# Attention ahead of a gated mixture of experts: smaller first loads, batch 0 partly transposed on TensorE, batch 1's transposes ahead of the first weights, adds in two alternating accumulators

## The chip, the core and the metric

One Trainium2 chip; the kernel runs on one of its cores. The metric is the device time of one execution in microseconds (us). Runs of one kernel differ by some tenths of a per cent.

## What is computed

Grouped-query attention over 8 batches (16 query heads, 4 key and value heads, 384 positions, 64 columns each), whose result is the input `x` (3072 x 1024) of a two-level gate: one of 4 groups, then one of 4 experts in it, each expert with two 1024 x 1024 matrices. Cut to what matters:

```python
scores = scale * np.matmul(q, k.transpose(0, 1, 3, 2))
attn = np.exp(scores - np.max(scores, axis=-1, keepdims=True))
attn = attn / (np.sum(attn, axis=-1, keepdims=True) + 1e-09)
x = np.matmul(attn, v)                      # per batch and head
g_idx = np.argmax(x @ w_group, axis=1)      # group, with its softmax weight
e_idx = np.argmax(xg @ w_expert[g], axis=1) # expert in the group, likewise
out[tok_idx] = combined[:, None] * (np.maximum(xg @ w1[g, e], 0.0) @ w2[g, e])
```

## The kernel before, in words

The program goes batch by batch. A batch's attention (`Attn.run`) has 24 units, six per key head `g`. A unit has four score products into one of two "s" tiles of PSUM (`score`, L256), an exp on ScalarE (L262, into a tile `e` of 128 x 768 f32), four value products (`pv`, L275, into an "o" tile), and an add on VectorE into the group's running sum (`tail`, L288): `es = es + e[u]`, five adds in a row on one tile. `score` runs two units ahead of `pv`. After a group its outputs are copied to `xT` (ScalarE, or VectorE for group 1). There are nine buffers for `e`.

Keys and queries must lie transposed. Of batch 0, the first half of the keys and the first query group are cast and transposed on TensorE (`first_scores`, L223 and L228) and the rest by DMA transposes on SP's queue (`trans_q` L122, `trans_k` L127). Of later batches all is transposed by DMA: `before_attention(b)` issues those of batch b + 1. Queries are loaded and cast by POOL's queue (L91), keys and values by SP's (L87, L96); a copy of the keys with each column doubled (`dup_k`, L115) is made by POOL in a single buffer.

Behind the attention of batch b comes `block(b)`: the expert of batch b - 1 (`ffn_h` L486: four pairs of hidden columns with a ReLU each; `ffn_y` L495) on TensorE, and around it for batch b the sums over keys (`reduce_keys` L321 on VectorE, `sums` L330 on TensorE and a reciprocal), the normalisation (`normalise`, L340 and L345 on VectorE), casts, and the gate (`gate_logits` L361, `gate_softmax`). The gate also guesses the expert that most tokens of batch b + 1 will want, from the mean of its values (`sum_v` L102 on VectorE, `guess_mean` L372), so that its weights can be requested early: `pick` reads the choice into a register on POOL and requests both matrices (L439, L442), 2 MB each as written. For batch 0 this guess is made inside its own attention, behind units 1 to 4, and batch 1's transposes are issued behind unit 5. Batch 1's attention carries batch 0's sums, normalisation and gate between its units. A loop at the end serves tokens that chose otherwise; it runs zero times here.

The order on every engine is the order in which the program is written; nothing is reordered. Each queue is served in order too: what stands behind a waiting instruction waits with it. The dictionaries given to `Attn.run` say behind which unit a step stands:

```python
at[0].run({
    1: [first_guess],
    2: [do(guess, 0)],
    4: [first_pick, do(prepare_k, 1)],
    5: [do(before_attention, 0)],
}, at[1])
```

## Time and profile before

| | |
|---|---|
| median of three runs | 440.46 us (439.91 to 441.97) |
| the profiled execution | 440.67 us |
| its span, first to last instruction | 439.0 us |
| busy, share of the span | TensorE 85%, VectorE 74%, ScalarE 55%, POOL 9% |
| mean granted TensorE clock | 0.97 of full speed |
| moved by transfers | 78.06 MB, mean 178 GB/s |

The profile shows one execution. Times within it count from the start of its span. Busy shares are means over stages with different limits, so the timeline of each engine is of more use here: it lists instructions in order, with the idle time of the engine ahead of an instruction and what ended that idle time, in brackets. PE is TensorE, DVE is VectorE, ACT is ScalarE; a queue is named with a q (SPq). A number L288 is a line of the kernel.

### The profile page before, as it was taken

How to read it: one execution, taken by the hardware profiler on the slowest of the kernel's cores; microseconds unless marked ns; L12 is line 12 of the kernel's file. 1: busy time of each engine (PE TensorE's matmuls, PEld its weight loads, DVE VectorE, ACT ScalarE, POOL GpSimd, SP SyncE). 2: the span in 40 equal slices, each digit the busy share in tenths (PEclk: the TensorE clock that was granted, in tenths of full speed). 3: DMA queues.
4: the chain of work that ended last, by engine and by line, in shares of the span. 5: the costliest groups of instructions: out<-in, count | busy, mean ns of one | idle time of the engine just before them, and what ended most of it. 6: DMA issues, size and time to landing. Idle time of an engine off the chain costs nothing.

```text
span 439.0 us, 8662 instructions
## 1 busy us (share of the span) xinstructions
PE 372.0 (85%) x3491; PEld 193.9 (44%) x3491; DVE 325.0 (74%) x509; ACT 242.7 (55%) x323; POOL 39.2 (9%) x52
## 2 busy tenths in 40 slices
PE   2895067587989999998999898999999899989993
PEld 1352033143445444554455444544455545544551
DVE  3689229999669994999499975999499949995321
ACT  3276057451659534973589265953497358926220
POOL 5030020040010010100210021001010001000000
PEclk9999578898999999999999999999999999999998
DMA  8949999249979999899969998999989946971524
GB/s 205 210 69 192 205 190 170 74 84 235 210 225 184 196 218 264 148 192 208 261 155 206 193 216 209 210 186 230 259 141 184 215 103 144 221 137 48 169 49 98
DMA packets 73050, 78.06 MB, mean 178 GB/s; under 512 B 37769, under 2 KB 52105, under 8 KB 73009
## 3 DMA queue, kind: packets, MB, share of 16 engines
q0 software_dynamic: 24736, 39.65, 53.2%
q1 hardware_dynamic: 47920, 37.36, 35.2%
q8 instruction: 28, 0.46, 0.4%
q10 hardware_dynamic: 352, 0.48, 0.4%
q14 instruction: 14, 0.11, 0.1%
HBM read 89.21 MB, written 18.87 MB: 246 GB/s over the span
## 4 chain that ended last, share of the span: by engine, by line
DVE 37%; PE 37%; issue 8%; ACT 8%; DMA 5%; SPq 2%; POOL 1%; DVEq 0%; POOLq 0%; ACTq 0%
DVE e L288 24%; PE ps_s L495 12%; PE ps_s L486 10%; ACT e L262 6%; DVE red L321 5%; DMA qT<-q_raw 4%; PE ps_o L495 4%; PE ps_o L275 3%; PE ps_o L361 2%; SPq L127 2%; DVE xT L294 1%; DVE vsum L102 1%; PE ps_o L486 1%; PE ps_s L256 1%; ACT ot L510 1%
## 5 line engine op out<-in xcount | busy, mean ns | idle before, releaser
L288 DVE TENSOR_TENSOR e<-e 128x768 f32<-128x768 f32 x160 | 154.8, 975 | 33.3 <-ACT xT L296 15.5
L262 ACT ACTIVATE e<-ps_s 128x768 f32<-128x768 f32 x192 | 148.0, 819 | 37.1 <-PE ps_s L256 31.9
L275 PE MATMUL ps_o<-e,v_raw 64*64 64x384 f32 x1536 | 162.7, 498 | 0.6 <-ACT e L262 0.2
L256 PE MATMUL ps_s<-qT,kT 64*64 64x384 bf16 x768 | 71.0, 339 | 27.4 <-DMA qT<-q_raw 17.5
L486 PE MATMUL ps_s<-xb,w 128*128 128x384 bf16 x480 | 82.3, 330 | 0.0
L275 PEld LDWEIGHTS ps_o<-e,v_raw 64*64 64x64 f32 x1536 | 63.3, 137 | 28.5 <-issue 17.3
L256 PEld LDWEIGHTS <-kT 64*64 64x64 bf16 x768 | 32.8, 108 | 75.1 <-issue 70.5
L486 PEld LDWEIGHTS <-w 128*128 128x128 bf16 x512 | 49.5, 99 | 37.0 <-issue 5.9
L488 ACT ACTIVATE hT<-ps_s 128x768 bf16<-128x768 f32 x30 | 24.3, 810 | 61.8 <-PE ps_s L486 61.8
L495 PE MATMUL ps_s<-w,hT 128*128 128x512 bf16 x248 | 55.5, 379 | 0.0
L495 PEld LDWEIGHTS <-hT 128*128 128x128 bf16 x384 | 36.1, 98 | 43.6 <-ACT hT L488 1.9
L349 ACT CAST xb<-xT 128x768 bf16<-128x768 f32 x32 | 26.3, 829 | 15.6 <-DVE xT L345 15.6
L345 DVE TENSOR_TENSOR xT<-xT,rb 128x768 f32<-128x768 f32 x32 | 31.8, 994 | 1.6
L495 PE MATMUL ps_o<-w,hT 128*128 128x512 bf16 x136 | 32.2, 379 | 0.0
L340 DVE STREAM_TRANSPOSE rb<-inv 128x768 f32<-128x768 f32 x32 | 31.3, 977 | 1.0
L321 DVE TRANSPOSE_TENSOR_REDUCE red<-e 128x24 f32<-128x768 f32 x32 | 28.7, 948 | 0.0
L296 ACT COPY xT<-ps_o 128x768 f32<-128x768 f32 x24 | 19.1, 796 | 7.8 <-PE ps_o L275 7.8
L514 ACT ACTIVATE ot<-ps_s,we 128x1024 f32<-128x1024 f32 x14 | 15.6, 1115 | 12.6 <-PE ps_s L495 12.6
L439 POOL DMA_DIRECT2D w<-in_moe_w_dram x8 | 7.1, 883 | 172.4 <-DVE cw_all L430 118.9
L102 DVE TENSOR_REDUCE vsum<-v_raw 128x256 bf16<-128x1536 f32 x8 | 22.1, 2761 | 0.0
L416 ACT ACTIVATE ex<-sh 128x24 f32<-128x24 f32 x8 | 1.8, 223 | 33.4 <-DVE sh L411 33.4
L91 POOL DMA_DIRECT2D q_raw<-in_q_dram x7 | 6.2, 881 | 153.9 <-DMA qT<-q_raw 153.9
(95 smaller groups left out, 159.7 us busy)
## 6 DMA issues: line engine op xcount, KB each, us to landing
w<-in_moe_w_dram POOLq DMA_DIRECT2D x16, 2048.0 KB, 21.6
out_dram<-ot SPq DMA_DIRECT2D x42, 256.0 KB, 5.5
v_raw<-in_v_dram SPq DMA_DIRECT2D x16, 384.0 KB, 6.6
xb_scratch<-xb SPq DMA_DIRECT2D x8, 768.0 KB, 6.4
q_raw<-in_q_dram POOLq DMA_DIRECT2D x7, 768.0 KB, 11.8
k_raw<-in_k_dram SPq DMA_DIRECT2D x7, 384.0 KB, 4.1
out_dram<-ot SPq DMA_DIRECT2D x12, 128.0 KB, 2.4
w<-in_q_dram POOLq DMA_DIRECT2D x3, 192.0 KB, 9.1
```

The source lines that it names most:

```text
L102: nc.vector.tensor_reduce(out=t.rearrange("p (h d) -> p h d", d=D), in_=vraw[b].rearrange("p h (c d) -> p h d c", c=NC), axis=AX.X, op=ALU ...
L256: nc.tensor.matmul(out=sT[r * H2:(r + 1) * H2, s, :S], lhsT=kT[b][s * D:(s + 1) * D, (g // 2) * NC + c, ks], rhs=qT[b][s * D:(s + 1) * D, ...
L262: nc.scalar.activation(e.rearrange("p t (s x) -> p s t x", s=2), sT[:, :, :S].rearrange("p s (t x) -> p s t x", t=2), ACT.Exp, scale=scale)
L275: nc.tensor.matmul(out=oT[t * D:(t + 1) * D, r, :S], lhsT=vraw[b][r * H2:(r + 1) * H2, g, c * D:(c + 1) * D], rhs=self.e[u][r * H2:(r + 1) ...
L288: nc.vector.tensor_add(out=es, in0=es, in1=self.e[u])
L321: nc.vector.tensor_reduce(out=red[b][:, g].rearrange("p t j -> p (t j)"), in_=ess[b][g].rearrange("p t (j x) -> p (t j) x", x=32), axis=AX ...
L340: nc.vector.transpose(out=rb.rearrange("p k (j x) -> p (k j) x", x=32), in_=inv[b][:, ks].rearrange("p k j -> p (k j)").unsqueeze(2).to_br ...
L345: nc.vector.tensor_mul(out=x, in0=x, in1=rb)
L349: nc.scalar.copy(out=xb[b][:, ks, :], in_=xT[b][:, ks, :])
L486: nc.tensor.matmul(out=h[:, jj, :S], lhsT=w1[:, kq, (f0 + jj) * P:(f0 + jj + 1) * P], rhs=x[:, kq, :], start=(kq == 0), stop=(kq == KQ - 1))
L488: nc.scalar.activation(hT[:, f0:f0 + 2, :], h[:, :, :S], ACT.Relu)
L495: nc.tensor.matmul(out=y[:, nh, :], lhsT=hT[:, f, c * P:(c + 1) * P], rhs=w2[:, f, nh * HALF:(nh + 1) * HALF], start=(f == 0), stop=(f == ...
```

## The change

Four things are done. First, the start: of the keys, the first half is loaded first, and of the values the first group; the second half of the keys and batch 1's keys and values are loaded behind them (`load_v0`). POOL builds the identity before it requests queries. ScalarE runs an exp on a constant at once (`early`). TensorE multiplies a constant eight times (`warm`). The first query group is cast, transposed and copied in two halves on two engines, and the second query group is transposed on TensorE as well (`first_q1`, behind unit 3). Second, batch 1's transposes, in four pieces for the queries, are issued ahead of batch 0's choice, which moves from behind unit 4 to behind unit 16; the value means of batches 0 and 1 are made by TensorE from the values themselves (`guess_mean_pe`, twelve products of 128 x 128 f32 with a column of ones) instead of VectorE's `sum_v`. Third, the adds run in two accumulators, `e[z]` and `e[z + 2]`, that are added together one unit later; there are twelve buffers for `e`, and one instead of two for `xT` (batch 1's lies in a buffer of `w1`). Fourth, `block`: the third pair of hidden columns stands ahead of the sums, `sum_v` behind the normalisation, the guess ahead of the logits; the two matrices are requested separately (batch 1's first one only in block 1); and the last output rows of a batch are scaled and stored behind unit 1 of the next attention (`late`).

```diff
-    epool = ctx.enter_context(tc.tile_pool(name="exp", bufs=9))
+    epool = ctx.enter_context(tc.tile_pool(name="exp", bufs=12))
...
-    for gp in range(2):
-        nc.sync.dma_start(out=k0f[:, gp], in_=rows(k[0])[:, gp])
...
+    def load_v0(g0, g1):
+        for r in range(2):
+            nc.sync.dma_start(out=vraw[0][r * H2:(r + 1) * H2, g0:g1],
+                              in_=v[0, g0:g1].rearrange("h (p c) d -> p h (c d)", c=NC))
...
+    onesb = cpool.tile([P, 4 * P], BF16)
+    nc.vector.memset(onesb, 1.0)
+    nc.sync.dma_start(out=k0f[:, 0], in_=rows(k[0])[:, 0])
     for m in range(KG):
         nc.scalar.dma_start(out=q0f[:, m], in_=rows(q[0])[:, m])
-    load_v(0)
-    wraw = stage[:NE // 2 * 5, 16 * NQ:16 * NQ + 2 * Eg * P].bitcast(F32)
...
-    for g in range(1, Hkv):
-        nc.gpsimd.dma_start(out=qraw[0][:, KG * g:KG * (g + 1)],
-                            in_=rows(q[0])[:, KG * g:KG * (g + 1)])
+    early = gpool.tile([P, 1], F32, name="early")
+    nc.scalar.activation(early, onesb[:, :1], ACT.Exp)
     id128f = cpool.tile([P, P], F32)
     make_identity(nc, id128f)
     id128b = cpool.tile([P, P], BF16)
     nc.gpsimd.tensor_copy(out=id128b, in_=id128f)
+    for g in range(1, Hkv):
+        nc.gpsimd.dma_start(out=qraw[0][:, KG * g:KG * (g + 1)],
+                            in_=rows(q[0])[:, KG * g:KG * (g + 1)])
+    load_v0(1, Hkv)
+    nc.sync.dma_start(out=k0f[:, 1], in_=rows(k[0])[:, 1])
+    load_k(1)
+    load_v(1)
     load_q(1)
...
+    def trans_pe(dst, src, n, which, eng, lo=0):
+        pt = ps_tile(which, [P, 16, P], BF16)
+        for i in range(n):
+            nc.tensor.transpose(out=pt[:, i, :], in_=src(i), identity=id128b)
...
     def first_scores():
         new_kT(0)
         new_qT(0)
...
-        dup_k(nc.gpsimd, kd, k0f, 1)
-        trans_q(0, 1, 2)
-        trans_k(0, kd, 1, 2)
-        trans_q(0, 2, 3)
-        trans_q(0, 3, 4)
+        kds[0] = new_kd()
+        warm = ps_tile("o")
+        for i in range(8):
+            nc.tensor.matmul(out=warm[:, i % 2, :], lhsT=onesb[:, :P], rhs=onesb, start=True,
+                             stop=True)
+        dup_k(nc.vector, kds[0], k0f, 0)
+        nc.scalar.copy(out=qraw[0][:, 0], in_=q0f[:, 0])
+        nc.vector.tensor_copy(out=qraw[0][:, 1], in_=q0f[:, 1])
+        trans_pe(kT[0][:, :NC, :], lambda i: kds[0][:, i].rearrange("p s d -> p (s d)"), NC, "s",
+                 nc.vector)
+        for m in range(KG):
+            trans_pe(qT[0][:, SC * m:SC * (m + 1), :], lambda i: q_block(SC * m + i), SC, "so"[m],
+                     (nc.scalar, nc.vector)[m])
+        dup_k(nc.gpsimd, kds[0], k0f, 1)
+
+    def first_q1(which):
+        trans_pe(qT[0][:, KG * SC:2 * KG * SC, :], lambda i: q_block(KG * SC + i), KG * SC, which,
+                 nc.vector)
...
+        def add(self, u, v_):
+            nc.vector.tensor_add(out=self.e[u], in0=self.e[u], in1=self.e[v_])
+
         def tail(self, u):
             b = self.b
             g, c = u // NC, u % NC
-            if c == 0:
-                ess[b][g] = self.e[u]
-                return
-            es = ess[b][g]
-            nc.vector.tensor_add(out=es, in0=es, in1=self.e[u])
+            z = u - c
+            if c == 0 and g:
+                self.add(z - NC, z - NC + 2)
+            elif c in (1, 3):
+                self.add(u - 1, u)
+            elif c >= 4:
+                self.add(z + 2 * (c - 4), u)
             if c == NC - 1:
+                ess[b][g] = self.e[z]
+                if g == Hkv - 1:
+                    self.add(z, z + 2)
                 if b not in xT:
-                    xT[b] = xpool.tile([P, KQ, S], F32, name="xT")
+                    if b == 1:
+                        w = wpool.tile([P, KQ, F], BF16, name="w1")
+                        xT[b] = w.rearrange("p a f -> p (a f)").bitcast(F32)[
+                            :, :KQ * S].rearrange("p (a n) -> p a n", n=S)
+                    else:
+                        xT[b] = xpool.tile([P, KQ, S], F32, name="xT", bufs=1)
                 dst, src = xT[b][:, KG * g:KG * (g + 1), :], self.oT[g][:, :, :S]
-                if g == 1:
+                if g == 1 and b > 1:
                     nc.vector.tensor_copy(out=dst, in_=src)
                 else:
                     nc.scalar.copy(out=dst, in_=src)
...
+    def guess_mean_pe(b, pt):
+        pm = pt[:, 1, :Hkv]
+        for g in range(Hkv):
+            for i in range(SC):
+                nc.tensor.matmul(out=pm[:, g:g + 1], lhsT=vraw[b][:, g, i * P:(i + 1) * P],
+                                 rhs=ones1, start=(i == 0), stop=(i == SC - 1))
...
-        er = nc.gpsimd.value_load(e_i[0:1, 0:1], min_val=0, max_val=NE - 1)
-        wts[b] = fetch(er)
+        ers[b] = nc.gpsimd.value_load(e_i[0:1, 0:1], min_val=0, max_val=NE - 1)
+
+    def pick_w1(b):
+        w1s[b] = fetch1(ers[b])
+
+    def pick_w2(b):
+        w2s[b] = fetch2(ers[b])
...
+    gate_constants()
     first_scores()
     at = {0: Attn(0), 1: Attn(1)}
     at[0].start()
-    load_k(1)
-    load_v(1)
-    gate_constants()
     state = {}
 
-    def first_guess():
-        sum_v(0)
-        gate_matrix("x")
+    def first_trans():
+        trans_q(0, 2, 3)
+        trans_k(0, kds[0], 1, 2)
+        trans_q(0, 3, 4)
+        prepare_k(1)
+        new_qT(1)
+        new_kT(1)
+        trans_k(1, kds[1], 0, 2)
+        for g in range(Hkv):
+            trans_q(1, g, g + 1)
 
     def guess(b):
         state["pt"] = ps_tile("x")
-        state["vm"] = guess_mean(b, state["pt"])
+        state["vm"] = guess_mean_pe(b, state["pt"])
 
     def first_pick():
         gate_softmax(None, state["pt"], state["vm"])
         pick(0)
-
+        pick_w1(0)
+        pick_w2(0)
+
+    first_trans()
     at[0].run({
-        1: [first_guess],
-        2: [do(guess, 0)],
-        4: [first_pick, do(prepare_k, 1)],
-        5: [do(before_attention, 0)],
+        0: [do(gate_matrix, "x")],
+        1: [index_constants],
+        3: [do(first_q1, "x")],
+        13: [do(guess, 0)],
+        16: [first_pick],
     }, at[1])
...
     def first_gate():
-        state["pt"] = gate_logits(0, "x")
-        state["vm"] = guess_mean(1, state["pt"])
+        state["pt"] = ps_tile("x")
+        state["vm"] = guess_mean_pe(1, state["pt"])
+        gate_logits(0, state["pt"])
...
         state["w"] = gate_softmax(0, state["pt"], state["vm"])
         pick(1)
+        pick_w2(1)
...
-    ins.setdefault(12, []).append(do(sum_v, 1))
...
         moe_h(f, 0, "s")
         reduce_keys(b, range(Hkv))
         moe_h(f, 2, "s")
-        if not last:
-            sum_v(b + 1)
+        moe_h(f, 4, "s")
         sums(b, "o")
         normalise(b, 0)
-        moe_h(f, 4, "s")
         normalise(b, 1)
         cast(b, 0)
         moe_h(f, 6, "s")
...
         moe_y(f, 0, "s")
         cast(b, 2)
         cast(b, 3)
+        if not last:
+            sum_v(b + 1)
+        if b == 1:
+            pick_w1(1)
         moe_y(f, 1, "s")
-        pt = gate_logits(b, "o")
+        pt = ps_tile("o")
         vm = None if last else guess_mean(b + 1, pt)
+        gate_logits(b, pt)
         nc.sync.dma_start(out=xb_dram[b], in_=xb[b])
-        y = ffn_y(wts[f][1], hTs[f], 2, "o", (0,))
+        y = ffn_y(w2s[f], hTs[f], 2, "o", (0,))
         w = gate_softmax(b, pt, vm)
         if not last:
             pick(b + 1)
+            pick_w1(b + 1)
             at[b + 1] = Attn(b + 1)
             at[b + 1].score(0)
         w()
-        ffn_y(wts[f][1], hTs[f], 2, "o", (1,), y)
+        out_weights(b)
+        ffn_y(w2s[f], hTs[f], 2, "o", (1,), y)
         if not last:
+            pick_w2(b + 1)
             at[b + 1].score(1)
+            return do(y_out, f, 2, y, True)
         y_out(f, 2, y, True)
-        out_weights(b)
-
+
+    late = None
     for b in range(1, B):
         if b > 1:
             before_attention(b)
-            at[b].run({})
-        block(b)
+            at[b].run({1: [late]})
+        late = block(b)
 
```

Three places in the order of instructions show it. SP's queue from its start, before:

```order
L139 DMA w_84<-in_k_dram 128x384 x2
L96 DMA v_raw<-in_v_dram 64x4x384 x2
L122 DMA_TRANSPOSE qT<-w_84 128x6x128
L127 DMA_TRANSPOSE kT<-k_dup 128x6x128
L122 DMA_TRANSPOSE qT<-w_84 128x6x128 x2
L87 DMA k_raw<-in_k_dram 128x2x384
L96 DMA v_raw<-in_v_dram 64x4x384 x2
L127 DMA_TRANSPOSE kT<-k_dup 128x12x128
L122 DMA_TRANSPOSE qT<-q_raw 128x24x128
```

and now:

```order
L148 DMA w_84<-in_k_dram 128x384
L143 DMA v_raw<-in_v_dram 64x384 x2
L143 DMA v_raw<-in_v_dram 64x3x384 x2
L164 DMA w_84<-in_k_dram 128x384
L87 DMA k_raw<-in_k_dram 128x2x384
L96 DMA v_raw<-in_v_dram 64x4x384 x2
L122 DMA_TRANSPOSE qT<-w_84 128x6x128
L127 DMA_TRANSPOSE kT<-k_dup 128x6x128
L122 DMA_TRANSPOSE qT<-w_84 128x6x128
L127 DMA_TRANSPOSE kT<-k_dup 128x12x128
L122 DMA_TRANSPOSE qT<-q_raw 128x6x128 x4
```

The two loads of batch 1 moved ahead of all transposes, one query transpose of batch 0 is gone, and the key transpose stands one place further back. (`w_84` holds batch 0's queries and keys, `kT` of 12 blocks and `qT` from `q_raw` are batch 1's.)

VectorE in the block behind batch 2's attention, before, from the last adds into the normalisation:

```order
L288 TENSOR_TENSOR e<-e 128x768 x10
L321 TENSOR_REDUCE red<-e 128x24 x4
L102 TENSOR_REDUCE vsum<-v_raw 128x256
L333 RECIPROCAL inv<-ps_o_1543 128x96
L340 STREAM_TRANSPOSE rb<-inv 128x768
L345 TENSOR_TENSOR xT<-xT,rb 128x768
L340 STREAM_TRANSPOSE rb<-inv 128x768
```

and now, from the end of the normalisation into the gate:

```order
L387 TENSOR_TENSOR xT<-xT,rb 128x768
L382 STREAM_TRANSPOSE rb<-inv 128x768
L387 TENSOR_TENSOR xT<-xT,rb 128x768
L102 TENSOR_REDUCE vsum<-v_raw 128x256
L415 CAST vm<-ps_o_1695 128x2
L446 COPY gl<-ps_o_1695 128x80
```

The value sum (`vsum`) moved from ahead of the reciprocal to behind the normalisation's last multiplication; ahead of the reciprocal there is now nothing between it and the four reductions.

POOL after its first five instructions, before:

```order
L147 DMA w_84<-in_q_dram 128x2x384 x3
masks.py:197 MEMSET id128f 128x128
masks.py:199 ISA
masks.py:199 AFFINE_SELECT id128f<-id128f 128x128
L152 CAST id128b<-id128f 128x128
L91 DMA q_raw<-in_q_dram 128x8x384
```

and now:

```order
masks.py:197 MEMSET id128f 128x128
masks.py:199 ISA
masks.py:199 AFFINE_SELECT id128f<-id128f 128x128
L159 CAST id128b<-id128f 128x128
L161 DMA w_84<-in_q_dram 128x2x384 x3
L91 DMA q_raw<-in_q_dram 128x8x384
```

The three query requests moved from ahead of the identity to behind it.

## Rows read from the trace of the kernel before

**Rows 1.** Timeline, 0 to 30 us: start us, us, engine line op, releaser.

```profile
5.01 0.80 PE L223 MATMUL ps_s<-id128b,k_dup 128*128 128x128 bf16 x6 [5.01 <-POOL id128b L152]
5.21 1.28 ACT L220 ACT_TABLE_LOAD   x1 [5.21 <-DMA w<-in_q_dram]
...
9.11 0.85 PE L256 MATMUL ps_s<-qT,kT 64*64 64x384 bf16 x8 [0.89 <-ACT qT L231]
...
9.69 2.25 ACT L262 ACTIVATE e<-ps_s 128x768 f32<-128x768 f32 x3 [0.63 <-PE ps_s L256]
...
24.20 0.18 DVE L395 COPY gl<-ps_o 128x20 f32<-128x20 f32 x1 [1.18 <-PE ps_o L380]
...
27.13 0.15 DVE L458 CAST e_i<-ef 128x1 int32<-128x1 f32 x1
...
28.81 0.90 POOL L439 DMA_DIRECT2D w<-in_moe_w_dram  x1 [21.46 <-DVE e L288]
```

**Rows 2.** Timeline of the SP queue, 30 to 75 us.

```profile
39.10 17.33 SPq L122 DMA_TRANSPOSE qT<-q_raw  x1
...
68.39 4.37 SPq L122 DMA_TRANSPOSE qT<-q_raw  x1
```

**Rows 3.** Timeline of PE, 30 to 108 us.

```profile
58.56 0.53 PE L256 MATMUL ps_s<-qT,kT 64*64 64x384 bf16 x4 [17.52 <-DMA qT<-q_raw]
...
105.37 0.51 PE L330 MATMUL ps_o<-red,half 128*64 128x48 f32 x8 [3.11 <-DVE red L321]
```

**Rows 4.** Timeline of DVE, 30 to 108 us.

```profile
62.61 0.96 DVE L288 TENSOR_TENSOR e<-e 128x768 f32<-128x768 f32 x1 [15.47 <-ACT xT L296]
63.49 0.97 DVE L321 TRANSPOSE_TENSOR_REDUCE red<-e 128x24 f32<-128x768 f32 x1
...
83.27 2.79 DVE L102 TENSOR_REDUCE vsum<-v_raw 128x256 bf16<-128x1536 f32 x1
```

**Rows 5.** SP timeline; transfers, 8 to 18 us: issue, count, us to landing.

```profile
10.65 1.91 SPq L127 DMA_TRANSPOSE kT<-k_dup  x1
...
kT<-k_dup SPq DMA_TRANSPOSE x1, 7.9
```

**Rows 6.** PE timeline, 126 to 176 us: batch 2 and its block.

```profile
127.17 0.36 PE L256 MATMUL ps_s<-qT,kT 64*64 64x384 bf16 x4 [0.53 <-ACT e L262]
...
147.52 5.37 PE L486 MATMUL ps_s<-xb,w 128*128 128x384 bf16 x32
154.40 0.44 PE L330 MATMUL ps_o<-red,half 128*64 128x48 f32 x8 [1.51 <-DVE red L321]
...
167.05 1.50 PE L361 MATMUL ps_o<-xT,wg 128*32 128x384 f32 x16
169.14 0.19 PE L372 MATMUL ps_o<-onesb,vsum 128*128 128x1 bf16 x2 [0.60 <-ACT lgs L365]
...
170.92 0.74 PE L390 MATMUL ps_o<-mod,lgs 128*128 128x20 f32 x6
...
174.58 0.36 PE L256 MATMUL ps_s<-qT,kT 64*64 64x384 bf16 x4 [0.48 <-ACT e L262]
```

**Rows 7.** Timeline of PE and DVE, 362 to 412 us: the last batch.

```profile
364.95 0.36 PE L256 MATMUL ps_s<-qT,kT 64*64 64x384 bf16 x4 [0.48 <-ACT e L262]
...
392.18 0.44 PE L330 MATMUL ps_o<-red,half 128*64 128x48 f32 x8 [1.50 <-DVE red L321]
...
400.56 0.96 DVE L345 TENSOR_TENSOR xT<-xT,rb 128x768 f32<-128x768 f32 x1
...
404.76 1.50 PE L361 MATMUL ps_o<-xT,wg 128*32 128x384 f32 x16
```

**Rows 8.** Chain of waits, 135 to 150 us: start us, us, what.

```profile
141.61 0.97 DVE e L288
...
142.67 0.97 DVE e L288
```

**Rows 9.** Page, part 2: what the transfers moved, in 40 equal slices.

```profile
GB/s 205 210 69 192 205 190 170 74 84 235 210 225 184 196 218 264 148 192 208 261 155 206 193 216 209 210 186 230 259 141 184 215 103 144 221 137 48 169 49 98
```

66 lines of the change are left out of this document (34 added, 32 removed).

## The prediction

> **What bounds the kernel now.** I first read the timeline of each engine along the span, then the chain of waits and the transfers in the places where an engine stood still. Three stretches behave differently.
>
> The start: the two query parts land at 5.2, and only then does ScalarE load its table (1.28 us); cast, transposes and copy follow one another, so the first score stands at 9.11 [rows 1]. The chain to the first choice of an expert ends at 27.28, and the weights are requested at 28.81.
>
> The gap: batch 1's transposes are issued behind that request. Its queries (24 blocks) take SP 17.33 us from 39.10, whereas batch 2's, at 68.39 and without weights beside them, take 4.37 [rows 2]. TensorE stands still for 17.52 us until 58.56, and its first four scores then take 0.53 against 0.36 later [rows 3, 6]. From 62.61, after 15.47 us of rest, VectorE is what ends last: until batch 1's sums at 105.37 it has adds, reductions, normalisation, a value sum of 2.79 us and the gate, and TensorE waits 3.11 us for it [rows 3, 4].
>
> The repeated block: from the first value product of a batch to that of the next is (364.95 - 127.17) / 5 = 47.56 us [rows 6, 7]. In each, TensorE leads: 20.35 us of attention (127.17 to 147.52), hidden layer, a wait of 1.51 us for the reductions, and a wait of 0.60 before the guess [rows 6].
>
> **The change part by part.** The sum is made against the profiled execution: 440.67 us, span 439.0, so 1.67 around it; the median of the runs is 0.2 lower.
>
> *First score.* The table load leaves the path, and cast, transposes and copy work on halves on two engines. The path of 9.11 - 5.21 = 3.9 us [rows 1] becomes about 1.7 (half of 0.8 three times, and gaps). So 6.9 instead of 9.11; bounds 5.9 (the smaller transfers also land 1 us earlier) and 9.1 (no gain). The first value product follows 1.4 later (exp starts at 9.69, three take 2.25): 8.3.
>
> *Batch 0 up to the choice, now behind unit 16.* 17 units at 20.35 / 24 = 0.848 are 14.4. Put between them on TensorE: the gate matrix 1.4 (four transposes at the rate of six in 0.80 [rows 1], one f32 product, and two short VectorE copies ahead of that product, about 0.6), six query transposes 0.8 [rows 1] and 0.5 for the copy that the next score waits for, and the value means. Those are 12 f32 products; six rows of the nearest kind (f32, 128 columns of weights, few moving columns) take 0.74 [rows 6], so 24 rows are 3.0; bounds 2.0 and 4.4 (rows half as long again, as 0.53 is to 0.36). With 0.3 for the guess: 6.0. That makes 28.7.
>
> *Transfers of batch 0.* The second key half now stands on SP behind more loads and one query transpose. Before, it was issued at 10.65 and landed 7.9 later [rows 5]. Now the query transpose ahead of it needs the second query request instead of the first (0.39 MB more at 205 GB/s [rows 9], 1.9), and the identity is built ahead of these requests (three short POOL steps, 1.3 by my estimate): issue at 13.9, landed at 21.8. TensorE would want it in unit 10, at 8.3 + 8.5 + 2.7 = 19.5. A wait of 2.3; bounds 0 and 8 (all landing times half as long again). That makes 31.0.
>
> *Choice and weights.* The chain on VectorE takes 27.28 - 24.20 = 3.1 as before: 34.1. The weights go out at about 35.6, some 7 us later than before, but batch 1's transposes are then issued: they need k_dup free (21.8), two casts, and by the undisturbed row about 2.2 and 4.4 us of issue, so they are done by 33, ahead of TensorE's need at unit 22 (36). The 17.5 us gap goes. The weights' delay is hidden: 4.2 MB at some 200 GB/s [rows 9] are 21 us, and batch 0's hidden layer wants the first of them only at about 70.
>
> *Batch 1, where VectorE sets the pace.* What is late next is VectorE, held up by the choice: seven adds of batch 0 are left, 6.5, so 40.6. From there its work is that of 62.61 to 105.37, 42.8 us, with these differences: +0.9 (batch 0's first reduction was done earlier), -2.7 (the value sum became TensorE's products, hidden here), -0.9 (one copy of outputs moves to ScalarE), +1.0 (the value sum used to fill a wait for the gate's logits), and the adds. A dependent add starts 1.06 after its predecessor (141.61, 142.67), an instruction on other data 0.88 after it (62.61, 63.49) [rows 4, 8]; two alternating accumulators turn some five of the eight adjacent pairs here into independent ones: -0.9. So 40.2: sums of batch 1 at 80.8 instead of 105.37.
>
> Here the alternation meets a rule. The rows say 0.88 against 1.06 [rows 4, 8]. The Trainium skill, VectorE: DVE Perf Modes, section "The DRAIN you can't avoid", says that the next operation does not start until the pipe is empty and that it makes no difference whether semaphores stand between; by it the alternation would gain nothing. This case's trace speaks against it, with those two spacings (the page itself points to an exception for instructions that are not held). By the rows the alternation is worth 0.9 here and 0.7 in the seven adds; without it the sum below would be 1.6 higher.
>
> *The block.* The third pair of hidden columns moves ahead of the sums: the reductions end before TensorE needs them, so the wait of 1.51 goes. But the value sum moves behind the normalisation, and that is the next thing late. From the sums to the end of the normalisation is 400.56 + 0.96 - 392.18 = 9.34 [rows 7]; with 2.7 for the value sum the guess can start 12.05 after the sums. TensorE gets there after 10.5: from 154.40 to 167.05 it needed 12.65 with two column pairs, now one pair (2.6) less, and 0.5 more because a cast now stands ahead of the last ReLU. So TensorE waits 1.5 again, elsewhere. From the guess to the next batch's first product it was 174.58 - 167.05 = 7.53; the 0.60 goes, since the guess now precedes the logits: 6.93. The period: 20.35 + 3 x 2.6 + 0.05 + 12.05 + 6.93 = 47.2, against 47.56. Five periods gain 1.9. The faster adds gain nothing here: VectorE waits for the sums anyway. The transposes, now ahead of the last output rows on SP, start some 8 us earlier, in the block where they had slack.
>
> *The last block* has no value sum: 20.35 + 7.85 + 10.5 = 38.7 to the logits, before 404.76 - 364.95 = 39.8. What follows stays: 439.0 - 404.76 = 34.24.
>
> **Sum.** Sums of batch 1 at 80.8; + 12.05 + 6.93 = 99.8 (before 127.17); + 5 x 47.2 = 335.8; + 38.7 + 34.24 = 408.7; + 1.67 = 410.4, and 0.2 less for the median: **410 us**. Of the 30 us nearly all come from before 105.37. Its own range, with the bounds of the start, the wait in unit 10 and the means: 406 to 417.
>
> **The rivals.**
> *The start runs smoother.* No wait in unit 10 (2.3), first score at 5.9 (1.0), means at 2.3 us (0.7), no wait for the logits (1.0): 5 us less, 405. For it: the 7.9 is a landing time among all of batch 0's loads [rows 5]. Against: slices 1 and 2 of the transfer row already move 205 and 210 GB/s [rows 9], and batch 1's keys and values now join them.
> *Batch 1's transposes stay late.* More loads crowd into the first 20 us, k_dup has one buffer, so one late key transpose delays everything behind it; if qT comes to lie beside the weights it falls back from 4.4 to 17.33 [rows 2]. 13 more, less the 3 of slack at unit 22 (33 against 36): 10, so 420, with a gap on TensorE in unit 22. For it: the order of the requests hangs on a choice at 34 and transposes done by 33, which is close.
> *The adds do not get faster*, by the page's rule as a mechanism of this kernel: every add starts 1.06 after the last. 1.6 more: 412. The two spacings speak against it.
> *The transfers become the bound, and it is slower than before.* Per period some 9.7 MB move (mean 204 GB/s of slices 13 to 32 [rows 9], times 47.56 us). If the transposes, which now run against the output rows and the first of the weights, bring the rate below 9.7 MB / 53.3 us = 182 GB/s, the five periods take 6.1 us more each and the 30 us are gone; at 178, the mean of the whole row, 54.5 us and 446. Against it: single slices reach 264 and 261.
> That the change does not do what it says holds in part and is in the forecast: in the repeated block the alternating accumulators bring nothing.
>
> **How the numbers follow.** Forecast 0.50, smoother start 0.25, late transposes 0.15, no faster adds 0.06, transfers 0.04. A measurement of this kernel can tell about 0.5% from no change, 2.2 us. The first four cases are all faster than that, 0.96 together; I leave 0.95 there and move 0.01 to no change for a mixture of mishaps, and of the last case's 0.04 another 0.01, where the rate falls only to about 182: faster 0.95, same 0.02, slower 0.03. The range reaches from the smoother start with the smaller price of the first exchange, 400, to late transposes with all of their delay on the path, 424.
>
> **What would show it.** Right: first score near 7; no idle of TensorE over 5 us between 10 and 60; weights requested after the last query transpose of batch 1 at 33 to 38; sums of batch 1 near 81, with VectorE busy all the way from 41; adjacent adds at 0.88; in the blocks no wait at the sums, but one of 1 to 2 us at the guess for the value sum; a period of 47. Wrong: a gap in unit 22 on qT, or at the first hidden layer on the weights; a period under 46 or over 48.5; sums of batch 1 before 74 or after 92.

## The result and the profile after

The changed kernel takes 421.3 us (median of four runs, 418.1 to 425.7) against 440.5 before: 0.9534 of it, 95% interval [0.9452, 0.9616]. Predicted were 410, range 400 to 424. The profiled execution took 424.22, its span is 422.6. The ratio takes in a fifth execution, of 420.0. It and the ratios below leave out executions that took over 1.5% longer than the fastest of their kernel (here 425.7); where too few were left for an interval, only the median and the ends are given. The four of the changed kernel lie 1.8% apart, those of the kernel before beside them 0.5%; one part of that is the stall that the experiments take up.

Page of the changed kernel, parts 2 and 4, and behind it part 4 of the kernel before. TensorE has the largest share of the chain that ended last, where before it and VectorE had 37% each. Slices 16 and 17 of the transfers are low (62 and 147 GB/s).

```profile
PEclk9999687999999999899999999999999999999998
...
GB/s 199 241 105 148 232 192 176 222 228 271 164 170 196 229 250 62 147 200 237 283 118 189 188 298 173 144 197 187 306 196 200 213 177 82 229 142 51 174 41 112
...
PE 48%; DVE 25%; ACT 11%; issue 9%; DMA 4%; SPq 1%; POOL 0%; DVEq 0%; POOLq 0%; ACTq 0%
```
```profile
DVE 37%; PE 37%; issue 8%; ACT 8%; DMA 5%; SPq 2%; POOL 1%; DVEq 0%; POOLq 0%; ACTq 0%
```

Timeline of PE to the sums of batch 1 (start, duration, line, operation, tiles and shapes, number of products; in brackets the wait and what ended it):

```profile
7.06 0.59 PE L285 MATMUL ps_s<-qT,kT 64*64 64x384 bf16 x8 [0.37 <-ACT qT L238]
...
21.70 0.36 PE L285 MATMUL ps_s<-qT,kT 64*64 64x384 bf16 x4 [1.02 <-DMA kT<-k_dup]
...
25.06 2.84 PE L422 MATMUL ps_o<-ones,v_raw 128*128 128x1 f32 x24
...
47.14 0.67 PE L372 MATMUL ps_o<-red,half 128*64 128x48 f32 x8 [6.19 <-DVE red L363]
...
63.15 2.79 PE L402 MATMUL ps_o<-xT,wg 128*32 128x384 f32 x16 [2.03 <-DVE vm L425]
...
86.07 0.44 PE L372 MATMUL ps_o<-red,half 128*64 128x48 f32 x8 [0.50 <-DVE red L363]
```

Of [rows 1], the first score moved from 9.11 to 7.06; of [rows 3], the 17.52 us for qT are gone, and the sums of batch 1 moved from 105.37 to 86.07. Batch 1's transposes are now ahead of the weights. The SP and POOL queues:

```profile
24.92 1.41 SPq L127 DMA_TRANSPOSE kT<-k_dup  x1
26.42 5.95 SPq L122 DMA_TRANSPOSE qT<-q_raw  x4
```
```profile
35.33 0.90 POOL L490 DMA_DIRECT2D w<-in_moe_w_dram  x1 [10.44 <-DVE e L311]
...
37.95 3.12 POOL L115 CAST k_dup<-k_raw 128x768 bf16<-128x768 f32 x2
```

VectorE between the choice and the gate of batch 0, where [rows 4] stood:

```profile
33.65 0.15 DVE L514 CAST e_i<-ef 128x1 int32<-128x1 f32 x1
33.72 8.16 DVE L311 TENSOR_TENSOR e<-e 128x768 f32<-128x768 f32 x7
41.80 0.96 DVE L363 TRANSPOSE_TENSOR_REDUCE red<-e 128x24 f32<-128x768 f32 x1
...
62.94 0.15 DVE L425 CAST vm<-ps_o 128x4 bf16<-128x4 f32 x1
67.83 0.96 DVE L311 TENSOR_TENSOR e<-e 128x768 f32<-128x768 f32 x1 [4.74 <-PE ps_o L304]
69.62 0.24 DVE L446 COPY gl<-ps_o 128x80 f32<-128x80 f32 x1 [0.83 <-PE ps_o L431]
```

Seven adds take 8.16, and VectorE rests 4.74 + 0.83 for the gate of batch 0. The chain is this: the cast of the value means (vm) stands behind VectorE's normalisations and adds, the logits on TensorE wait 2.03 for that cast (PE, 63.15), and two units follow ahead of the gate. TensorE also slows down there: its granted clock is 0.50 to 0.53 of full speed (the lower of its two levels) from 61 to 68, in and behind that wait, and the logits take 2.79 instead of the 1.50 that they take in the blocks.

The block, timeline of PE: the guess of blocks 1 to 4, and a wait in batch 3. A wait put to "issue" is one in which the engine waited for nothing that the profile shows.

```profile
98.17 0.20 PE L412 MATMUL ps_o<-onesb,vsum 128*128 128x1 bf16 x2 [1.43 <-DVE vsum L102]
...
145.50 0.20 PE L412 MATMUL ps_o<-onesb,vsum 128*128 128x1 bf16 x2 [1.44 <-DVE vsum L102]
...
172.76 0.35 PE L285 MATMUL ps_s<-qT,kT 64*64 64x384 bf16 x2 [4.24 <-issue]
...
199.10 0.20 PE L412 MATMUL ps_o<-onesb,vsum 128*128 128x1 bf16 x2 [1.44 <-DVE vsum L102]
...
246.38 0.20 PE L412 MATMUL ps_o<-onesb,vsum 128*128 128x1 bf16 x2 [1.44 <-DVE vsum L102]
```

The wait at the sums [rows 6] is gone; one of 1.43 to 1.44 stands at the guess. The periods, counted from one guess to the next, are 47.33, 53.60, 47.28, 49.11 and 47.27. The two long ones cost 8.1 us against 47.3.

### The profile page after: what moved, and what is told of

Read it like the earlier page. It is cut to its first block, busy times and chain, and to the rows that moved or that the text cites. A ratio compares the mean times of both kernels' runs of the same rounds, so it can differ in the third digit from the quotient of the medians.

```text
span 422.6 us, 8740 instructions
## 1 busy us (share of the span) xinstructions
PE 374.3 (89%) x3553; PEld 200.7 (48%) x3553; DVE 314.4 (74%) x510; ACT 241.4 (57%) x326; POOL 40.7 (10%) x52
## 4 chain that ended last, share of the span: by engine, by line
PE 48%; DVE 25%; ACT 11%; issue 9%; DMA 4%; SPq 1%; POOL 0%; DVEq 0%; POOLq 0%; ACTq 0%
PE ps_o L304 13%; PE ps_s L547 12%; DVE e L311 9%; PE ps_s L556 6%; ACT e L291 5%; PE ps_o L556 5%; PE ps_s L285 5%; DVE vsum L102 4%; PE ps_o L402 3%; DVE rb L382 2%; DVE xT L387 2%; DMA kT<-k_dup 2%; DMA w<-in_q_dram 2%; ACT ot L575 2%; DVE red L363 1%
## 5 line engine op out<-in xcount | busy, mean ns | idle before, releaser
L311 DVE TENSOR_TENSOR e<-e 128x768 f32<-128x768 f32 x160 | 148.9, 975 | 17.3 <-PE ps_o L304 16.0
L291 ACT ACTIVATE e<-ps_s 128x768 f32<-128x768 f32 x192 | 145.8, 820 | 24.0 <-PE ps_s L285 21.3
L304 PE MATMUL ps_o<-e,v_raw 64*64 64x384 f32 x1536 | 158.2, 492 | 1.3 <-issue 1.3
L547 PE MATMUL ps_s<-xb,w 128*128 128x384 bf16 x480 | 80.8, 326 | 0.0
L304 PEld LDWEIGHTS ps_o<-e,v_raw 64*64 64x64 f32 x1536 | 64.4, 136 | 25.7 <-issue 18.3
L391 ACT CAST xb<-xT 128x768 bf16<-128x768 f32 x28 | 23.2, 830 | 20.7 <-DVE xT L387 20.7
L387 DVE TENSOR_TENSOR xT<-xT,rb 128x768 f32<-128x768 f32 x28 | 26.8, 958 | 1.4
L446 DVE COPY gl<-ps_o 128x80 f32<-128x80 f32 (+2 forms) x9 | 2.1, 232 | 30.8 <-PE ps_o L431 25.5
L338 ACT COPY xT<-ps_o 128x768 f32<-128x768 f32 x22 | 17.5, 795 | 6.7 <-PE ps_o L304 6.7
L375 DVE RECIPROCAL inv<-ps_o 128x96 f32<-128x96 f32 x8 | 6.1, 757 | 19.5 <-PE ps_o L372 19.5
L91 POOL DMA_DIRECT2D q_raw<-in_q_dram x7 | 6.2, 885 | 148.9 <-DMA qT<-q_raw 148.9
```

What stands on the lines that cost most here:

```text
L291: nc.scalar.activation(e.rearrange("p t (s x) -> p s t x", s=2), sT[:, :, :S].rearrange("p s (t x) -> p s t x", t=2), ACT.Exp, scale=scale)
L304: nc.tensor.matmul(out=oT[t * D:(t + 1) * D, r, :S], lhsT=vraw[b][r * H2:(r + 1) * H2, g, c * D:(c + 1) * D], rhs=self.e[u][r * H2:(r + 1) ...
L311: nc.vector.tensor_add(out=self.e[u], in0=self.e[u], in1=self.e[v_])
L387: nc.vector.tensor_mul(out=x, in0=x, in1=rb)
L391: nc.scalar.copy(out=xb[b][:, ks, :], in_=xT[b][:, ks, :])
L547: nc.tensor.matmul(out=h[:, jj, :S], lhsT=w1[:, kq, (f0 + jj) * P:(f0 + jj + 1) * P], rhs=x[:, kq, :], start=(kq == 0), stop=(kq == KQ - 1))
```

## The experiments

Each run alters the changed kernel by the edit shown or named; lines left out are marked with "...". The text behind each heading, as far as it is set off, was written before the run. Below, "sums" are the sums of batch 1 over keys; "after the choice" counts from the end of the cast e_i of batch 0, at 33.80 in the changed kernel.

**The changed kernel again.**

> The changed kernel once more, unaltered. In its first profile two of the six periods between value guesses were 53.6 and 49.1 us, four were 47.3; TensorE stood 4.24 us in the middle of a unit's scores with nothing that the profile shows to wait for. If that stall falls at random (a code or transfer hiccup), it stands elsewhere or is missing here, the undisturbed periods are again 47.2 to 47.4, and the times spread from 416 to 426. If it belongs to a place of the program, batch 3 has it again, near 173 us, with 4 us.

421.9 (417.96 to 426.31). Its profiled execution took 417.96: sums at 86.06, periods 47.37, 47.53, 48.92, 47.26, 47.27, no wait on issue over 0.3 us. So the stall is not there in every execution. The SP queue shows two ways of running in one execution, the transposes beside the weights (24.41) and without them (3.98):

```profile
147.07 5.89 SPq L127 DMA_TRANSPOSE kT<-k_dup  x1
155.99 24.41 SPq L122 DMA_TRANSPOSE qT<-q_raw  x1
...
194.39 4.55 SPq L127 DMA_TRANSPOSE kT<-k_dup  x1
199.69 3.98 SPq L122 DMA_TRANSPOSE qT<-q_raw  x1
```

**Value means of batch 1 at unit 8.**

```diff
+    def first_means():
+        state["vm"] = guess_mean_pe(1, ps_tile("x"))
...
         state["pt"] = ps_tile("x")
-        state["vm"] = guess_mean_pe(1, state["pt"])
         gate_logits(0, state["pt"])
...
-    ins.setdefault(13, []).append(first_gate)
-    ins.setdefault(15, []).append(first_softmax)
+    ins.setdefault(8, []).append(first_means)
+    ins.setdefault(14, []).append(first_gate)
+    ins.setdefault(16, []).append(first_softmax)
```

> The value means of batch 1 are taken at unit 8 into a PSUM tile of their own; the logits of batch 0 at unit 14, the softmax at 16. Theory: the 4.74 + 0.83 us in which VectorE waits for the gate of batch 0 come from the means that stand ahead of the logits in the same tile and from their cast, which is late in VectorE's row. Then some 4 us of them go (1.5 left), batch 1's sums come at 82 instead of 86.1, and the time is 4 us shorter than the changed kernel's. Rival: TensorE, at its lower speed after the 6.2 us wait for the reductions, is late by itself; then the wait only moves behind the softmax, the sums stay at 85 to 86 and the time is the same.

417.49 (415.19 to 418.71), ratio 0.947 [0.94, 0.9539]. This interval overlaps that of the changed kernel, so it is the trace that decides. VectorE's wait for the gate fell to one line:

```profile
67.44 0.24 DVE L446 COPY gl<-ps_o 128x80 f32<-128x80 f32 x1 [0.57 <-PE ps_o L431]
```

Sums came at 82.62, 47.3 after the choice instead of 52.3. The theory holds, with 5.0 where it said 4. The rival, that the wait only moves, falls; but TensorE's lower speed had its part in the price: here the granted clock is 0.99 to 1.00 from 52 to 72 and the logits take 1.50, where the changed kernel had 0.50 to 0.53 and 2.79. The edit also moves the gate back by one unit, which no run takes apart.

**Value sum right behind the reductions.**

```diff
         reduce_keys(b, range(Hkv))
+        if not last:
+            sum_v(b + 1)
         moe_h(f, 2, "s")
...
         cast(b, 3)
-        if not last:
-            sum_v(b + 1)
```

> The value sum of the next batch stands right behind the reductions again, ahead of the sums; the third pair of hidden columns stays ahead of the sums. Theory: two pairs of hidden columns (5.4 us) behind the first cover 3.8 us of reductions less what is done earlier and 2.8 of value sum, so no wait comes back at the sums, the wait of 1.43 at the guess goes in each block, the period falls from 47.3 to 45.9 and the time by 8 us (6 blocks by 1.43). Rival: the value sum pushes the reciprocal behind the sums and the normalisation back by as much as it did at the guess, so that a wait of 1 to 2 us stands at the gate's logits instead: period 47 to 47.5, the time the same.

424.1 (411.11 to 428.07): by time it tells nothing, and the profiled execution is the longest, 428.07. In it the wait at the guess is gone and the shortest period is 45.68, but others last 47.1 to 55.2, and TensorE waits 4.12 and 7.75 us for qT. The short period was seen again in the last runs.

**Alternation undone.**

```diff
-            if c == 0 and g:
-                self.add(z - NC, z - NC + 2)
-            elif c in (1, 3):
-                self.add(u - 1, u)
-            elif c >= 4:
-                self.add(z + 2 * (c - 4), u)
+            if c:
+                self.add(z, u)
...
-                if g == Hkv - 1:
-                    self.add(z, z + 2)
```

> Alternation alone undone: every add goes into the first tile of its group again, seven other edits stay. Theory: adjacent adds start 1.06 us apart instead of 0.88 to 0.91; the seven adds before batch 0's last reduction and the pairs in batch 1 cost 1.6 us more, so batch 1's sums come at 87.7 instead of 86.1; in the blocks no difference (period 47.3); time 1.6 us longer. By the rule that the next operation starts only when the pipe is empty, the spacing is 1.06 in both kernels and the time does not move. Rival on the other side: the last group's chain ends later in each block and comes back as a wait at the sums: 0.2 to 1 us in each of seven batches, 1 to 7 us more.

421.21 (419.49 to 423.27), 0.9543 [0.9477, 0.9608], as the changed kernel. Batch 2's adds on VectorE, chained and then alternating (changed kernel):

```profile
109.63 9.19 DVE L311 TENSOR_TENSOR e<-e 128x768 f32<-128x768 f32 x9
...
119.60 10.32 DVE L311 TENSOR_TENSOR e<-e 128x768 f32<-128x768 f32 x10
129.84 3.55 DVE L357 TRANSPOSE_TENSOR_REDUCE red<-e 128x24 f32<-128x768 f32 x4
```
```profile
108.94 4.55 DVE L311 TENSOR_TENSOR e<-e 128x768 f32<-128x768 f32 x5
...
117.15 6.29 DVE L311 TENSOR_TENSOR e<-e 128x768 f32<-128x768 f32 x7
...
127.21 3.55 DVE L363 TRANSPOSE_TENSOR_REDUCE red<-e 128x24 f32<-128x768 f32 x4
```

1.02 to 1.03 us an add against 0.90 to 0.91: the spacing is real. The Trainium skill, VectorE: DVE Perf Modes, section "The DRAIN you can't avoid", says that the next operation does not start until the pipe is empty. The alternating adds do not fit that; the section names an exception for an operation that is not held, and no run here shows whether it is at work.

It bought no time that can be told. In the block, reductions end at 130.8 instead of 133.4, and sums wait for neither. At the start two things oppose each other. Sums came 51.1 after the choice, 1.2 less than with alternation: the last add of a group stands behind the next group's first value product there, so with alternation seven adds are left behind the choice instead of six; and VectorE, sooner at the gate, waited longer (3.85 here, 5.57 there). But the choice itself came 1.8 later with chained adds, at 35.64, because three adds instead of two stand on VectorE ahead of the copy of the second query group. TensorE waits 2.36 for that copy, against 0.65 to 1.32 in the twelve other profiles here, and then has a granted clock of 0.57 from 18 to 21. With chained adds, and with the changed kernel:

```profile
16.71 0.36 PE L285 MATMUL ps_s<-qT,kT 64*64 64x384 bf16 x4 [2.36 <-DVE qT L240]
```
```profile
15.39 0.36 PE L285 MATMUL ps_s<-qT,kT 64*64 64x384 bf16 x4 [1.16 <-DVE qT L240]
```

Together the sums came at 86.76 instead of 86.07, 0.7 later where the theory said 1.6.

**Weights held until the transposes have landed.**

```diff
-            pick_w1(b + 1)
             at[b + 1] = Attn(b + 1)
...
-            pick_w2(b + 1)
...
+    def hold(b):
+        if b + 1 < B:
+            t = gpool.tile([P, 1], BF16, name="hold")
+            nc.gpsimd.tensor_copy(out=t, in_=qT[b + 1][:, 0, :1])
+        pick_w1(b)
+        pick_w2(b)
...
             before_attention(b)
+            hold(b)
             at[b].run({1: [late]})
```

> The changed kernel, with one thing more: from block 1 on, both weight requests for the next batch stand behind the issue of that batch's successor's transposes, and POOL first copies one column of that qT, so that no weights are requested before those transposes have landed. The weights are not needed before the block after next. Theory: the changed kernel has two ways of running. Where q_raw (one buffer) is loaded before the weights are requested, the two transposes take 8.5 us of SP; where not, they lie beside the weights, take 30 us, the next load of queries is late by as much, and so on; in that way the transfer rate falls to 35 to 58 GB/s for up to 16 us, TensorE stands 1 to 4 us on issue, and a period lasts 49 to 54 us instead of 47.3. Then here every transposition of queries from batch 4 on takes 4 to 5 us, all periods are 47.2 to 47.4, no wait on issue over 0.5 us is left, the times lie within 1.5 us of one another, and the time is 414 to 416. Rival: the long periods come from the mere amount of transfers (9.7 MB a period); then they stay, in number and size, and the time is 418 to 426, or longer, since the weights start later.

417.23 (415.55 to 418.33), 0.9423 [0.938, 0.9466]. Periods 47.34, 47.27, 47.28, 47.29, 47.27, transposes of queries 4.07 to 6.96 from batch 3 on, and no wait on issue over 0.3. The mechanism is as the theory has it. The fastest and the slowest execution lie 2.8 us apart instead of 8.4, where the theory said 1.5, and none took over 418.4; the median is 1 to 3 above its figure. In the profiled execution the choice came 1.5 later (see the last section), which would account for about that much.

Now the stall itself. Here are windows of the changed kernel: the stretch, its length, the busy time of PE, PEld, DVE, ACT and POOL with their instructions, then TensorE's granted clock, the DMA engines' busy share and GB/s. The queues are full (share above 1), the rate falls to 59 GB/s, and TensorE's granted clock is full until after the stop. Behind it stands the same stretch of time in the last kernel below, with held weights; it is not quite the same place of the program.

```profile
156.00:172.00 16.00, 12.40 (x178) 7.01 (x171) 13.87 (x16) 13.16 (x18) 0.78 (x1) 1.00 1.26 59
172.00:193.00 21.00, 19.80 (x146) 12.01 (x146) 13.43 (x15) 8.73 (x11) 0.00 (x0) 0.92 1.12 188
```
```profile
156.00:172.00 16.00, 15.95 (x172) 9.05 (x165) 15.76 (x17) 10.38 (x14) 5.00 (x6) 1.00 0.84 174
```

What does it wait for? Not for data: it stops between two matmuls of one unit. The same stops were seen in pairs: after 1501 weight loads of the program in the changed kernel (4.24 us) and with chained adds (4.03); after 1117 with the early value sum (0.84) and with the late key copy, below (5.26); after 2396 in the changed kernel (1.32) and with the early value sum (0.57). The last pair on PE:

```profile
272.58 0.55 PE L304 MATMUL ps_o<-e,v_raw 64*64 64x384 f32 x4 [1.32 <-issue]
```
```profile
270.06 0.55 PE L304 MATMUL ps_o<-e,v_raw 64*64 64x384 f32 x4 [0.57 <-issue]
```

A weight load and a matmul are two instructions, so the places are 768 and 1790 instructions apart. The page of the changed kernel lists two queues of kind "instruction". One has 29 packets with 0.48 MB, some 16.5 KB each; TensorE has 3553 products and as many weight loads, together 27.8 times 256, so I take that queue for TensorE's:

```profile
q8 instruction: 29, 0.48, 0.5%
```

The Trainium skill, Runtime: NRT & Kernel Launch, section "Instruction fetch mechanics", says that an engine's program is fetched in blocks of 256 instructions and that this is mostly hidden. By that 3 and 7 blocks are 768 and 1792 instructions, and the places fit within 2. The trace has the time of every packet of that queue, and it settles what the stop waits for. In the changed kernel a packet moved from 169.54 to 171.31, in the middle of the stop; the transfers from 169.4 to 171.4:

```profile
DMA packets 80, 0.12 MB, mean 60 GB/s; under 512 B 32, under 2 KB 32, under 8 KB 79
...
q8 instruction: 1, 0.02, 5.5%
```

All six stops end 1.3 to 1.6 us after the end of such a packet:

| kernel | packet ends | TensorE goes on |
|---|---|---|
| changed | 171.31 | 172.76 |
| changed | 271.27 | 272.58 |
| chained adds | 171.53 | 172.96 |
| early value sum | 126.25 | 127.74 |
| early value sum | 268.55 | 270.06 |
| late key copy | 157.99 | 159.56 |

Where the same three places were passed without a stop over 0.5 us, in these and the other traces with 29 packets, the packet had ended 1.6 to 7.4 us before the load that follows, with held weights 3.4 to 7.4. At the first stop it started 19.3 us behind the packet before it, in the second profile of this kernel 13.0. So the stop is an instruction block that came late; here it was not hidden. That the low rate makes it late is seen only from where it lies: stretches of 8 to 16 us that reach to the stops move 59 to 101 GB/s at a DMA share of 1.23 to 1.40. A stop of over 0.5 us was seen in four of the nine profiles with free weights and in none of the four with held ones. Transposes beside the weights do not always bring one: with the key copy on ScalarE, below, they took 22 to 34 us in all five blocks, and TensorE did not stop. Holding the weights also moves them against all other transfers, so that run does not single out the transposes.

**Batch 1's transposes behind the first weights, in the program's order alone.**

```diff
-        new_qT(1)
-        new_kT(1)
-        trans_k(1, kds[1], 0, 2)
-        for g in range(Hkv):
-            trans_q(1, g, g + 1)
...
-        16: [first_pick],
+        16: [first_pick, do(before_attention, 0)],
```

> Batch 1's key and query transposes are issued behind the first weights again, as before the change; k_dup is made early as in the changed kernel. Theory: the gap of 17.5 us is what the change removed. The transposes then take 17 to 20 us from 37 on, TensorE stands for 15 to 18 us at unit 22, VectorE's stretch of batch 1 (44 us) starts late by as much less the 5 us by which the choice holds it anyway, batch 1's sums come at 97 to 100 instead of 86, and the time is 11 to 14 longer. Rival: VectorE, which has seven adds and four reductions of batch 0 to do meanwhile, hides most of the gap: 5 us or less.

420.67 (417.2 to 433.97); sums at 85.44. Neither theory is put to the test: SP does not wait for POOL's requests, so the transposes went out at 24.69 and 26.20 all the same.

**Batch 1's key copy behind the choice.** As the last one, and besides

```diff
-        prepare_k(1)
-        16: [first_pick, do(before_attention, 0)],
+        16: [first_pick, do(prepare_k, 1), do(before_attention, 0)],
```

> The key copy of batch 1 on POOL stands behind the choice and the two weight requests again, as before the change, and batch 1's transposes behind that; the loads stay early. The run with the transposes alone moved told nothing: SP does not wait for POOL's requests, so they went out at 24.7 to 30.8 all the same. Theory: what removed the gap is that the key copy on POOL no longer queues behind the choice. Here the copy comes at 37 to 40, the transposes lie beside the weights (17 us for the queries, as before the change), are done at about 60, TensorE stands some 24 us at unit 22, and batch 1's sums come at 99 to 103 instead of 86: 13 to 17 us longer. Rival: VectorE needs until 47 for batch 0's adds and reductions in any case, and the loads are early, so that the transposes take 6 to 10 us: sums at 88 to 90, 2 to 4 us longer.

453.65 (450.24 to 455.09), 1.0241 [1.0193, 1.0289]: some 2% slower than the kernel before, so the gain is gone and more. TensorE and VectorE:

```profile
67.62 0.54 PE L285 MATMUL ps_s<-qT,kT 64*64 64x384 bf16 x4 [29.46 <-DMA qT<-q_raw]
```
```profile
72.31 0.96 DVE L311 TENSOR_TENSOR e<-e 128x768 f32<-128x768 f32 x1 [26.59 <-PE ps_o L304]
```

The queries' transposes took 15.47 from 50.03; sums came at 115.45, 29.4 later. The theory is right in its mechanism, but the price was 32 instead of 13 to 17 us. With the choice now behind unit 16, hardly anything covers the gap: VectorE itself rests 26.59 until value products behind it. So without the key copy that POOL makes ahead of the choice the rest of the change loses time: the later choice depends on that copy.

**One of eight warming products.**

```diff
-        for i in range(8):
+        for i in range(1):
```

> Of the eight products at the very start, whose result nobody reads, one is left. Theory: in the kernel before, the first scores took 0.53 and the value products 1.49 for eight until 24 us, half speed; in the changed one 0.33 to 0.36 and 0.81 from 7 us on, and the eight products keep TensorE busy from 1.6 to 5.2 us ahead of that. Without them the first six to ten units take 1.6 instead of 0.85, the wait of 1.02 for the keys in unit 10 is used up, the choice comes 3 to 6 us later (37 to 40 instead of 33.8), and the time is 3 to 5 us longer. Rival: the transposes and scores bring the speed up by themselves within a unit or two, and the wait in unit 10 covers it: less than 1 us.

420.54 (417.74 to 428.91), 0.946 [0.9414, 0.9507]: no difference to be told. Units took 1.6 us each until 15.8 and 0.81 from there; the score that waits for the keys came at 23.06, without a wait, instead of 21.70. So the slow units cost 2.4 us, of which the wait of 1.02 covers its part and 1.4 is left: the theory's 3 to 5 is too much, and the rest is below what these times tell. (The granted clock is given as 1.00 for both stretches; only the durations show the slow units.) The choice came at 36.8, but with a later dip of the clock (last section) that other runs have too.

**Batch 2's key copy on ScalarE.**

```diff
-    prepare_k(2)
+    kds[2] = new_kd()
+    for gp in range(2):
+        a = slice(gp * NC, (gp + 1) * NC)
+        nc.scalar.copy(out=kds[2][:, a], in_=kraw[2][:, gp].rearrange(
+            "p (c d) -> p c d", d=D).unsqueeze(2).to_broadcast([P, NC, 2, D]))
```

> The changed kernel with batch 2's key copy on ScalarE instead of POOL. Theory: the seven adds ahead of batch 0's first reduction took 8.16 us, 1.17 each, because POOL copied keys beside them (3.12 us, from 37.95 to 41.07; the two adds in it took 1.5 each, those outside 0.9 to 1.0). Then here they take 6.4 to 6.7, POOL's 3.1 us are gone, and batch 1's sums come 1.5 us earlier, 84.5; time 1.5 us shorter. Rival: alternating adds with waits for the value products cost that much by themselves: 8 us again, and no difference.

417.21 (415.87 to 418.67), 0.9432 [0.9395, 0.9469].

```profile
36.74 6.41 DVE L311 TENSOR_TENSOR e<-e 128x768 f32<-128x768 f32 x7
```

6.41 instead of 8.16, and sums 49.3 after the choice instead of 52.3. The adds are 1.75 of these 3.0 us; the rest was not traced. The choice came 3.0 later here, with the dip of the last section, so the sums stood at 86.15 where the theory had 84.5. In the changed kernel POOL's two copies took 3.12, beside no adds 1.60: each slowed the other. The Trainium skill, SBUF — State Buffer, section "SBUF: two separate sides", says that a VectorE operation with two SBUF inputs and a GpSimd one that reads SBUF shut each other out for a whole instruction. These rows agree: the adds lost 1.75 us beside the copies, and the copies 1.52 beside the adds.

**Three together, and a fourth.** Held weights, early means and early value sum:

> Held weights, value means of batch 1 at unit 8, value sum right behind the reductions, together. Theory: the three act in different places, so their gains add: 4 us at batch 1's sums (82), the period 45.7 instead of 47.3 in all six (the run with the early value sum alone had 45.68 where nothing disturbed it), and no disturbed period: 416 less 4 less 9.6, some 402 to 404. Rival: at 45.7 a period asks 9.7 MB / 45.7 us = 212 GB/s; if the transfers cannot give that, the period stays at 47 or more and the time at 410 to 414, with waits of TensorE on qT or of SP on q_raw.

407.41 (403.08 to 411.72), 0.9133 [0.9085, 0.9181] from the two shortest, 403.08 and 405.03, which is about what the theory said; it did not have the other two, 409.78 and 411.72. In the profile, of 409.78, the period behind block 1 is 46.70 and the later ones are 45.66 to 45.68. The same with block 1's value sum kept late:

> Held weights and value means at unit 8; the value sum right behind the reductions only from block 2 on, in block 1 behind the normalisation. With all three everywhere, block 1 took 13.9 us from sums to guess (12.1 in the changed kernel): VectorE sets the pace there and the early value sum of 2.8 us stood before the reciprocal. Theory: that 1.6 goes, batch 1's sums at 82.6, guess 12.2 later, all five later periods 45.7, so 401 to 403, against 403.1 and 405.0 of the undisturbed runs with all three. Rival: the lower clock in batch 1 (0.50 to 0.81 from 48 to 64 us there) and not the value sum made block 1 long: then 403 to 406, as before.

409.14 (406.26 to 410.94), 0.925 [0.9213, 0.9287]: above both figures. From sums to guess block 1 took 12.64 instead of 13.9, but TensorE waited 1.98 for the value sum, its clock was 0.87 and 0.70 from 96 to 104, and it took 36.87 instead of 35.23 to the next sums. With the early value sum everywhere and the key copy on ScalarE:

> Held weights, value means at unit 8, value sum right behind the reductions in every block, and batch 2's key copy on ScalarE. Counted from the choice of batch 0 (the cast of the index, 33.7 to 36.7 in the runs so far, by whether TensorE's clock falls to 0.50 after the value means), batch 1's sums came 52.3 later in the changed kernel, 47.3 with the early means, 49.3 with the key copy on ScalarE, 49.8 with the first three together. Theory: the two add: 45 to 47 here, batch 1's sums at 80 to 83, later periods 45.7, time 403 to 406, 1.5 to 3 less than the three together (407.4). Rival: with the choice out of the way and the key copy gone, TensorE or ScalarE sets the pace of batch 1, and only one of the two gains counts: sums 47 to 50 after the choice, time 406 to 409.

402.5 (400.51 to 404.1), 0.9146 [0.9119, 0.9174] of before: better than both kernels, by 19 us than the changed one. All six executions lie within 3.6 us; by ratio it is not to be told from the two shortest of the three together. Sums at 80.26, 46.8 after the choice, so the two gains add in part. Blocks on PE, no wait left at the guess:

```profile
137.71 0.19 PE L412 MATMUL ps_o<-onesb,vsum 128*128 128x1 bf16 x2
...
183.40 0.19 PE L412 MATMUL ps_o<-onesb,vsum 128*128 128x1 bf16 x2
...
229.09 0.19 PE L412 MATMUL ps_o<-onesb,vsum 128*128 128x1 bf16 x2
```

This answers the early value sum's rival: the period is 45.68 to 45.74, so no wait of 1 to 2 us came in its place. Here the alternation should be of use: VectorE rests only 0.44 between the value sum and the reciprocal (at 173.38, batch 3), and with chained adds the reductions would end 2.6 later. That is an estimate; no run has the value sum early with chained adds.

## Why the prediction was right, and where it was not

The sign and the main mechanism were right, the time 11 us too low. That the range of 400 to 424 holds 421.3 is partly luck: the forecast's own bounds were 406 to 417, and the upper end was the price of late transposes, which did not come. A sign of being wrong did come, a period over 48.5, twice. Two terms of the sum were too small, one gain did not show, and one loss stood only under a rival with 0.04.

- *First score, choice, weights.* 7.06 for 6.9; wait in unit 10 1.02 for 2.3; means 2.84 for 3.0; choice 33.8 for 34.1; weights 35.33 for 35.6; transposes done at 32.4 for 33, no gap in unit 22. Right, and the late key copy shows that this is where the gain is. That the choice came out so close is in part two misses that cancel: TensorE came to unit 10 at 20.7 for 19.5, and waited 1.3 less there.
- *"Seven adds of batch 0 are left, 6.5".* Failed by 1.7: 8.16. I priced them by [rows 4, 8] alone and did not see that batch 2's key copy on POOL falls on them. Without it they took 6.41. As the choice was 0.3 early, the reduction came at 41.80 for 40.6.
- *"-2.7 (the value sum became TensorE's products, hidden here)" and "+1.0 (the value sum used to fill a wait for the gate's logits)".* Failed: VectorE rested 5.57 for 1.0, so the products were not hidden. The wait is not what the value sum left open. The value products that replaced it brought their own chain: their cast waits in VectorE's row, the logits, in the same PSUM tile, wait for the cast, and TensorE's granted clock is at its lower level behind that wait. With the means at unit 8, 5.0 us went. VectorE's stretch to the sums was 44.3 for 40.2, so sums at 86.07 for 80.8.
- *The alternation's 1.6 at the start.* Its spacing was right (0.90 to 0.91 for 0.88), its gain was not: undone, sums came 0.7 later in the profile, as a later choice and a shorter stretch behind it oppose each other, and no time was lost that can be told.
- *The block.* Wait at the guess 1.43 for 1.5, period 47.3 (without the two long ones) for 47.2, sums to the row of scores just ahead of the first value product 19.5 for 18.98 (the rows 127.17 and 364.95 that I called value products are such scores), last sums to logits 10.59 for 10.5. Right.
- *"The transfers become the bound".* I gave it 0.04 as a rate over a whole period (182 GB/s). The resource was right, the form was not: the transposes ahead of the output rows often start together with the weights, for 16 us the rate is 59 GB/s, and a block of TensorE's instructions comes late (a stop of 4.24, and one of 1.32). Two periods were 8.1 us longer. Of the 6.3 of the longer one the stop is 4.24; the granted clock of 0.78 to 0.79 from 172 to 180, behind the stop, goes with the rest.

The profiled execution adds up: 410.4 predicted + 1.2 (reduction later, by the adds) + 4.1 (stretch) + 0.5 (to the first product) + 8.1 (long periods) = 424.3, measured 424.22; the other terms are off by 0.5 and less and cancel. The execution of 417.96 has 2.0 of longer periods instead: 418.2. Of the rivals, the smoother start came in unit 10 only, and the late transposes did not come; the adds did get faster, against the rival that says they do not, and changed no time that can be told.

What stays open: why the rate falls so low where transposes and weights start together, and that this is what delays an instruction block, were not isolated. The smaller first loads, the second query group on TensorE and the new order in the block were not undone one by one; their shares are read from rows. And why the kernel before, whose query transposes mostly lay beside the weights (18.3 us, median of seven), kept 192 to 218 GB/s between 150 and 210 us and shows no stop, was not tried.
